# The gated stage of a fused three-layer kernel: six units of 384 tokens in place of four batches of 576 in halves of 288

## The chip, the cores and the metric

The kernel runs on one core of one Trainium2 chip. The metric is the device time of one execution in microseconds (us), the median of the runs. Engines are named as in the profile: PE is TensorE (matmuls), PEld its weight loads, DVE is VectorE, ACT is ScalarE, POOL is GpSimd, SP is the engine that issues most of the DMAs.

## The reference, cut to what matters

Three layers follow each other: an attention over 32 memory slots, a mixture of experts, and the gated layer that the change is about. There are 4 batches of 576 tokens; a token has 512 features, and the gated layer has 1024 hidden ones. `x` below is the output of the mixture of experts.

```python
h = np.maximum(x @ w_in, 0.0)                          # (4, 576, 1024)
hp = np.concatenate([zeros, h, zeros], axis=1)         # one zero row before and behind each batch
conv_out = sum(conv_w[k] * hp[:, k:k + 576, :] for k in range(3))
gate = 1.0 / (1.0 + np.exp(-conv_out))
out = h * gate @ w_out
```

The convolution runs along the tokens: a token's gate needs the hidden values of the token before it and of the token behind it in the same batch. At a batch's border the missing neighbour counts as zero.

## The kernel before

The first half (to about 205 us) computes attention and experts and leaves the experts' outputs, not yet multiplied by their gate probabilities, in DRAM (`ydram`, by batch, features on partitions, tokens along the rows; the probabilities are in `pdram`). The second half is `gated`. Nearly all products are of float32 numbers split into a high and a low part (`split`: ACT copies the high part, DVE or POOL subtracts), so each product is three matmuls (`matmul3`, L166).

`gated` walks over the 4 batches. For a batch it does the following.

- The batch's `y` (128 x 4 x 576) is loaded ahead by SP (`load_y`, L897), with the row of probabilities (`load_p`, L891). `split_y` multiplies (L905, DVE) and splits it into `yh` and `yl` (L153 ACT, L154 DVE). The pool of `y` has two buffers, `yh` and `yl` have one each, so a batch's split waits until the matmuls of the batch before have read them, and the next load but one waits for the split.
- For each of 8 groups `f` of 128 hidden features it computes `pi` = w_in x y: 4 feature blocks x 3 split terms x 2 halves of 288 tokens = 24 matmuls with 288 columns (L166). `pi` has two PSUM buffers.
- ACT takes `pi` through Relu into `ht` (L1050) and scales it into `ct` (L1052); DVE adds the two neighbours with two scalar_tensor_tensor instructions (L1053, L1055, 575 columns each); ACT takes the sigmoid (L1030); DVE multiplies (L1031, "mult" below); ACT copies the high part of `g` (L153), and DVE subtracts for the low part (L154), POOL for f = 3, 4 and 6 (`ON_POOL`). POOL also copies the last 64 tokens of the batch into `tail` (L1036), so that two batches' tails share one chunk of 128 tokens. `ht` and `ct` share 6 buffers (tag `cv`).
- The second product `po` (L1071) takes chunks of 128 tokens: 24 matmuls of 512 columns each (8 f x 3 terms). First the parts f = 0 to 5 of three chunks, then f = 6 and 7 of these, then whole chunks: 4 chunks for even batches, 5 for odd ones (the shared tail). ACT copies each chunk out (L1097), SP stores it (L1099 to L1102). The very last chunk goes into its own PSUM tile `last` and is copied out in two halves behind the branch (L1119).

The branch `tc.If(any_more > 0)` holds a second pass (`gated` with `scaled=True`) for batches in which more than one expert occurs; it isn't taken here. Instructions of one engine run in the order in which they stand in its queue. In `gated` that order is chosen at build time by a planner that simulates the engines; only the matmuls of the first batch's `pi` are kept in program order.

## Time and profile before

| | before |
|---|---|
| median of 3 runs | 411.95 us (411.86 to 412.09) |
| the profiled execution | 411.12 us |
| its span, first to last instruction | 409.4 us |
| PE busy | 401.6 us (98%) |
| DVE, ACT, POOL busy | 277.0, 221.4, 74.3 us |
| DMA | 69.04 MB, 169 GB/s in the mean |

A page of the profile has six parts; the share of busy time by engine is part 1, the span in 40 slices part 2, the costliest groups of instructions part 5. A timeline lists instructions in order of time: start, duration, engine, line, operation, output<-input, shape, and in square brackets how long the engine stood idle before it and on whom it waited. Merged rows carry a count (x12). A matmul's duration is longer than the distance to the next one, since matmuls are pipelined: for PE, the distance of starts is the cost. A table by windows lists, for each stretch, its length and each engine's busy time with the number of instructions, then the granted clock (1.00 is 2.4 GHz), the DMA share and GB/s.

### The profile page before, as it was taken

The page shows a single profiled execution, that of the slowest core. Times are in us where ns is not written, and L with a number is a line of the kernel's source. Part 1 is how long each engine was busy: PE and PEld are TensorE (multiplying, and loading weights), DVE is VectorE, ACT ScalarE, POOL GpSimd, SP SyncE. Part 2 cuts the span into 40 slices and gives each one's busy share as a digit, 9 for nine tenths or more (in the row PEclk, how much of TensorE's full clock was granted, in tenths as well). Part 3 has the DMA queues.
Part 4 walks back from the last instruction along what each step waited for, and adds up shares of the span by engine and source line. Part 5 has one row for each costly group of instructions (what it writes and reads, how often), then busy time and mean ns, then how long its engine had stood idle before and what let it go on. Part 6 is the DMA issues. An engine that isn't in the chain of part 4 may idle for free. (4 is left out here: it accounts for less than half of the span.)

```text
span 409.4 us, 8381 instructions
## 1 busy us (share of the span) xinstructions
PE 401.6 (98%) x3334; PEld 369.0 (90%) x3335; DVE 277.0 (68%) x513; ACT 221.4 (54%) x420; POOL 74.3 (18%) x123
## 2 busy tenths in 40 slices
PE   7999999999999999999999999999999999999995
PEld 6768989899998998999999988998889988999884
DVE  2679898897787986697989980688205793077600
ACT  4456567564666466465757732677215773267411
POOL 1000201402122211320102520033200232014300
PEclk9999999999999999999999999999999999999999
DMA  7999979999384949938630032000120000200022
GB/s 271 330 373 404 386 250 355 406 415 382 94 300 159 365 173 403 391 142 206 199 142 2 0 117 102 2 0 2 43 68 20 2 1 0 104 2 0 3 80 56
DMA packets 23904, 69.04 MB, mean 169 GB/s; under 512 B 3280, under 2 KB 4048, under 8 KB 23856
## 3 DMA queue, kind: packets, MB, share of 16 engines
q1 hardware_dynamic: 20272, 56.88, 38.8%
q0 software_dynamic: 3584, 11.54, 7.2%
q8 instruction: 28, 0.46, 0.4%
q14 instruction: 20, 0.16, 0.1%
HBM read 52.08 MB, written 16.33 MB: 167 GB/s over the span
## 5 line engine op out<-in xcount | busy, mean ns | idle before, releaser
L166 PE MATMUL py<-h,wb 128*128 128x288 f32 x768 | 105.3, 296 | 0.0
L166 PEld LDWEIGHTS py<-h,wb 128*128 128x128 f32 x768 | 102.4, 189 | 0.8 <-issue 0.3
L166 PE MATMUL pi<-yh,wi 128*128 128x288 f32 x512 | 90.7, 296 | 0.0
L1071 PE MATMUL po<-wo,g 128*128 128x512 f32 x360 | 84.2, 389 | 0.0
L1071 PEld LDWEIGHTS po<-wo,g 128*128 128x128 f32 x360 | 67.0, 188 | 13.1
L166 PEld LDWEIGHTS pi<-yh,wi 128*128 128x128 f32 x512 | 76.6, 189 | 0.9
L1053 DVE SCALAR_TENSOR_TENSOR ct<-ht,convw,ct 128x575 f32<-128x575 f32 x32 | 30.9, 965 | 53.0 <-ACT ct L1052 52.9
L166 PE MATMUL pi<-yl,wi 128*128 128x288 f32 x256 | 54.8, 296 | 0.0
L166 PE MATMUL ph<-att,vh 128*128 128x288 f32 x256 | 53.1, 301 | 0.2 <-DVE h L794 0.2
L1036 POOL CAST tail<-g 128x128 fp32r<-128x128 f32 x32 | 22.4, 702 | 122.7 <-DVE g L154 122.1
L878 POOL DMA_DIRECT2D ydram<-ys x32 | 17.6, 548 | 144.2 <-ACT ys L877 124.3
L166 PEld LDWEIGHTS ph<-att,vh 128*128 128x128 f32 x256 | 40.6, 188 | 3.4 <-issue 1.1
L166 PEld LDWEIGHTS pi<-yl,wi 128*128 128x128 f32 x256 | 41.2, 189 | 0.0
L1050 ACT ACTIVATE ht<-pi 128x576 f32<-128x576 f32 x32 | 20.8, 651 | 35.1 <-PE pi L166 35.1
L166 PE MATMUL ph<-att,vl 128*128 128x288 f32 x128 | 37.6, 295 | 0.0
L793 ACT ACTIVATE h<-ph 128x288 fp32r<-128x288 f32 x64 | 25.6, 408 | 17.7 <-PE ph L166 17.5
L794 DVE SCALAR_TENSOR_TENSOR h<-ph,h 128x288 fp32r<-128x288 f32 x64 | 27.9, 450 | 10.8 <-ACT h L793 10.6
L1097 ACT ACTIVATE ot<-po 128x512 f32<-128x512 f32 x17 | 9.5, 599 | 43.4 <-PE po L1071 43.4
L1031 DVE TENSOR_TENSOR ct<-ht,ct 128x576 f32<-128x576 f32 x32 | 27.2, 849 | 7.5 <-ACT ct L1030 7.5
L877 ACT ACTIVATE ys<-py 128x288 f32<-128x288 f32 x32 | 13.1, 409 | 35.4 <-PE py L166 16.4
L1055 DVE SCALAR_TENSOR_TENSOR ct<-ht,convw,ct 128x575 f32<-128x575 f32 x32 | 28.4, 887 | 0.4
L153 ACT ACTIVATE g<-ct 128x576 fp32r<-128x576 f32 x32 | 21.6, 679 | 12.6 <-DVE ct L1031 12.6
(231 smaller groups left out, 513.2 us busy)
## 6 DMA issues: line engine op xcount, KB each, us to landing
kv<-in_kv SPq DMA_DIRECT2D x16, 512.0 KB, 8.1
q<-in_q SPq DMA_DIRECT2D x8, 576.0 KB, 9.5
ydram<-ys POOLq DMA_DIRECT2D x32, 144.0 KB, 5.1
y<-ydram SPq DMA_DIRECT2D x4, 1152.0 KB, 5.8
out<-ot SPq DMA_DIRECT2D x15, 256.0 KB, 2.0
ph<-in_phi SPq DMA_DIRECT2D x8, 288.0 KB, 6.8
adram<-at POOLq DMA_DIRECT2D x8, 288.0 KB, 6.3
wa_1r<-in_w SPq DMA_DIRECT2D x4, 512.0 KB, 5.3
```

Source lines behind the costliest of these rows:

```text
L153: pin(nc.scalar.activation(hi, src, AF.Copy))
L166: pin(nc.tensor.matmul(ps, st, mv[:, cols], start=i == 0, stop=i == len(terms) - 1))
L793: nc.scalar.activation(t[:, 0, :], ps, AF.Relu)
L794: low = nc.vector.scalar_tensor_tensor(t[:, 1, :], ps, 0.0, t[:, 0, :].bitcast(F32), ALU.max, ALU.subtract)
L877: nc.scalar.activation(yt, ps, AF.Copy)
L878: stored.append(nc.gpsimd.dma_start(ydram[b, d, :, half(hf)], yt).ins)
L1031: slow(f"gm.{f}").tensor_tensor(ct, ht, ct, ALU.mult)
L1036: nc.gpsimd.tensor_copy(tail[:, f, :, to:to + 64], t[:, :, 512:576].bitcast(F32))
L1050: nc.scalar.activation(two(ht), halves(ps), AF.Relu)
L1053: nc.vector.scalar_tensor_tensor(ct[:, 1:], ht[:, :S - 1], convw[:, 0, f:f + 1], ct[:, 1:], ALU.mult, ALU.add)
L1055: nc.vector.scalar_tensor_tensor(ct[:, :S - 1], ht[:, 1:], convw[:, 2, f:f + 1], ct[:, :S - 1], ALU.mult, ALU.add)
L1071: last_product[:] = [nc.tensor.matmul(ps[:, cols], st[sp], w[:, mp, f % 2, cols], start=f == 0 and i == 0, stop=f == 7 and i == 2).ins]
```

## The change

The 4 x 576 = 2304 tokens are cut into 6 units of 384 tokens, three to every two batches. The first unit of three lies in one batch, the second crosses the border (192 tokens of each), the third lies in the second batch. A unit reads 386 columns: its 384 tokens and two neighbours (`spans`). So a unit has 8 x 12 matmuls of 386 columns in place of 8 x 24 of 288, and exactly 3 chunks of 128 tokens, with no tail. In the crossing units (1 and 4) the load is two DMAs for `y` and two for the probabilities, and each of the two DVE neighbour additions becomes two pieces of 191 or 192 columns, since tokens at the border have no neighbour across it. The last unit holds two chunks and the separate `last` tile; the hint for the branch stands behind the f = 0 to 5 parts of those two.

```diff
@@ -23,6 +23,7 @@
 B, H, S, D, M = 4, 8, 576, 64, 32
 DM, E, F = 512, 8, 1024
 HALF = S // 2
+UT, UW = 384, 386
 EPS = 1e-9
 FAR = 3e38
 
@@ -891,27 +892,36 @@
             nc.sync.dma_start(p, pdram[ds(e + 8 * b, 1), :].to_broadcast([128, S]))
             return p
 
-        def load_y(b, e):
-
-            y = state.tile([128, 4, S], F32, tag="ay", name=f"y{b}")
-            nc.sync.dma_start(y, ydram[b].rearrange("d p s -> p d s"))
-            return y, load_p(b, e, b) if e is not None else None
-
-        def split_y(b, yp, yh, yl):
+        def spans(u):
+
+            b = 2 * (u // 3)
+            return ([(b, 0, 0, UW)], [(b, 383, 0, 193), (b + 1, 0, 193, UW)], [(b + 1, 190, 0, UW)])[u % 3]
+
+        def load_y(u, scaled):
+
+            y = state.tile([128, 4, S], F32, tag="ay", name=f"y{u}")
+            p = None if scaled else late[1].tile([128, S], F32, tag="p", bufs=2, name=f"p{u}")
+            for b, at, a, z in spans(u):
+                nc.sync.dma_start(y[:, :, a:z], ydram[b].rearrange("d p s -> p d s")[:, :, at:at + z - a])
+                if not scaled:
+                    nc.sync.dma_start(p[:, a:z], pdram[ds(expert(b) + 8 * b, 1), at:at + z - a].to_broadcast([128, z - a]))
+            return y, p
+
+        def split_y(u, yp, yh, yl):
             y, p = yp
             for d in range(4):
                 if p is not None:
-                    with tc.issue_after(hidden_low[-1]) if b == 0 else contextlib.nullcontext():
-                        nc.vector.tensor_tensor(y[:, d, :], y[:, d, :], p, ALU.mult)
-                split(yh[:, d, :], yl[:, d, :], y[:, d, :])
-
-        def y_parts(b):
-            return [late[1].tile([128, 4, S], F32R, tag=t, bufs=1, name=f"{t}{b}") for t in ("yh", "yl")]
+                    with tc.issue_after(hidden_low[-1]) if u == 0 else contextlib.nullcontext():
+                        nc.vector.tensor_tensor(y[:, d, :UW], y[:, d, :UW], p[:, :UW], ALU.mult)
+                split(yh[:, d, :], yl[:, d, :], y[:, d, :UW])
+
+        def y_parts(u):
+            return [late[1].tile([128, 4, UW], F32R, tag=t, bufs=1, name=f"{t}{u}") for t in ("yh", "yl")]
 
         ys0 = []
 
         def load_first():
-            ys0.append(load_y(0, expert(0)))
+            ys0.append(load_y(0, False))
 
         def split_first():
             ys0.append(y_parts(0))
@@ -1008,99 +1018,85 @@
 
 
         def gated(gp, nm, scaled=False):
-            def first(b):
-                return None if scaled else expert(b)
 
             wo.clear()
             for j in range(4):
                 stage_out(j)
             ys = y_parts(0) if scaled else ys0[1]
             if scaled:
-                split_y(0, load_y(0, None), *ys)
-            tail = None
-            for b in range(B):
+                split_y(0, load_y(0, True), *ys)
+            for u in range(6):
                 yh, yl = ys
                 gs = []
-                if b + 1 < B:
-                    yn = load_y(b + 1, first(b + 1))
-                if b % 2 == 0:
-                    tail = gp.tile([128, 8, 2, 128], F32R, tag="tail", bufs=1, name=f"tail{b}")
-                to = 64 * (b % 2)
+                if u < 5:
+                    yn = load_y(u + 1, scaled)
+
+                o = u % 3
+                own = slice(o, o + UT)
+                lefts = ([(1, UT)], [(0, 192), (193, UT)], [(0, UT)])[o]
+                rights = ([(0, UT)], [(0, 191), (192, UT)], [(0, UT - 1)])[o]
+
                 def gate(f, ht, ct):
                     nc.scalar.activation(ct, ct, AF.Sigmoid)
-                    slow(f"gm.{f}").tensor_tensor(ct, ht, ct, ALU.mult)
-                    t = gp.tile([128, 2, S], F32R, tag="g", name=f"g{nm}{b}_{f}")
-
-                    def finish():
-                        split(t[:, 0, :], t[:, 1, :], ct, slow(f"gs.{f}"))
-                        nc.gpsimd.tensor_copy(tail[:, f, :, to:to + 64], t[:, :, 512:576].bitcast(F32))
-
+                    slow(f"gm.{f}").tensor_tensor(ct, ht[:, own], ct, ALU.mult)
+                    t = gp.tile([128, 2, UT], F32R, tag="g", name=f"g{nm}{u}_{f}")
                     gs.append(t)
-                    return finish
+                    return lambda: split(t[:, 0, :], t[:, 1, :], ct, slow(f"gs.{f}"))
 
                 before = None
                 for f in range(8):
                     fs = slice(f * 128, (f + 1) * 128)
-                    ps = banks(f"pi{b}_{f}")
-                    matmul3([(ps[:, hf, :HALF], half(hf)) for hf in range(2)],
+                    ps = banks(f"pi{u}_{f}")[:, 0, :UW]
+                    matmul3([(ps, slice(0, UW))],
                             [((wi[kc][:, 0, fs], wi[kc][:, 1, fs]), (yh[:, kc, :], yl[:, kc, :])) for kc in range(4)],
-                            tc.keep_in_program_order if b == 0 else lambda ins: ins)
+                            tc.keep_in_program_order if u == 0 else lambda ins: ins)
                     finish = gate(*before) if before else lambda: None
-                    ht = lp.tile([128, S], F32, tag="cv", name=f"ht{b}_{f}")
-                    nc.scalar.activation(two(ht), halves(ps), AF.Relu)
-                    ct = lp.tile([128, S], F32, tag="cv", name=f"ct{b}_{f}")
-                    nc.scalar.activation(ct, ht, AF.Copy, scale=convw[:, 1, f:f + 1])
-                    nc.vector.scalar_tensor_tensor(
-                        ct[:, 1:], ht[:, :S - 1], convw[:, 0, f:f + 1], ct[:, 1:], ALU.mult, ALU.add)
-                    nc.vector.scalar_tensor_tensor(
-                        ct[:, :S - 1], ht[:, 1:], convw[:, 2, f:f + 1], ct[:, :S - 1], ALU.mult, ALU.add)
+                    ht = lp.tile([128, S], F32, tag="cv", name=f"ht{u}_{f}")[:, :UW]
+                    nc.scalar.activation(ht, ps, AF.Relu)
+                    ct = lp.tile([128, S], F32, tag="cv", name=f"ct{u}_{f}")[:, :UT]
+                    nc.scalar.activation(ct, ht[:, own], AF.Copy, scale=convw[:, 1, f:f + 1])
+                    for k, by, pieces_of in ((0, -1, lefts), (2, 1, rights)):
+                        for a, z in pieces_of:
+                            nc.vector.scalar_tensor_tensor(ct[:, a:z], ht[:, o + a + by:o + z + by], convw[:, k, f:f + 1],
+                                                           ct[:, a:z], ALU.mult, ALU.add)
                     finish()
                     before = f, ht, ct
                     while len(wo) < 4 and f >= WO[len(wo)]:
                         wo.append(w2_piece(f"wo{len(wo)}", slow(f"wo.{len(wo)}")))
                 gate(*before)()
-                if b + 1 < B:
-                    ys = y_parts(b + 1)
-                    split_y(b + 1, yn, *ys)
-
-                def product(ps, c, fr, cols=slice(0, 512)):
+                if u < 5:
+                    ys = y_parts(u + 1)
+                    split_y(u + 1, yn, *ys)
+
+                def product(ps, c, fr):
                     for f in fr:
                         w = wo[f // 2].rearrange("p s (i d) -> p s i d", i=2)
-                        st = [gs[f][:, s, c * 128:(c + 1) * 128] if c < 4 else tail[:, f, s, :] for s in range(2)]
+                        st = [gs[f][:, s, c * 128:(c + 1) * 128] for s in range(2)]
                         for i, (sp, mp) in enumerate(((0, 0), (0, 1), (1, 0))):
-                            last_product[:] = [nc.tensor.matmul(ps[:, cols], st[sp], w[:, mp, f % 2, cols],
+                            last_product[:] = [nc.tensor.matmul(ps, st[sp], w[:, mp, f % 2, :],
                                                                 start=f == 0 and i == 0, stop=f == 7 and i == 2).ins]
 
-                chunks = [0, 1, 2] + [4] * (b % 2) + [3]
-                pss = {c: bank(f"po{b}_{c}") for c in chunks[:3]}
-                for c in chunks[:3]:
-                    product(pss[c], c, range(0, 6))
-                for c in chunks:
-                    if c in pss:
-                        product(pss[c], c, range(6, 8))
-                    elif b < B - 1 or c != chunks[-1]:
-                        pss[c] = bank(f"po{b}_{c}")
-                        product(pss[c], c, range(8))
-                    else:
-
-                        if not scaled:
-                            ps2_cm.__exit__(None, None, None)
-                            last_cm.append(tc.tile_pool(name="ps3", bufs=1, space=PSUM))
-                            pairs.append(last_cm[0].__enter__())
-
-                            with tc.issue_after(last_product[0]):
-                                tc.mark_branch_hint_location("more", engines=[ENG.PE])
-                            last_block.append(pairs[-1].tile([128, 512], F32, tag="last", name="last"))
-                        product(last_block[0], c, range(8))
-                        continue
-                    ot = gp.tile([128, 512], F32, tag="ot", bufs=4, name=f"ot{b}_{c}")
-                    nc.scalar.activation(ot, pss[c], AF.Copy)
-                    if c < 4:
-                        nc.sync.dma_start(out[b, c * 128:(c + 1) * 128, :], ot)
-                    else:
-                        nc.sync.dma_start(out[b - 1, 512:576, :], ot[0:64])
-                        nc.sync.dma_start(out[b, 512:576, :], ot[64:128])
-
+                pss = [bank(f"po{u}_{c}") for c in range(3 if u < 5 else 2)]
+                for c, ps in enumerate(pss):
+                    product(ps, c, range(0, 6))
+                if u == 5 and not scaled:
+
+                    with tc.issue_after(last_product[0]):
+                        tc.mark_branch_hint_location("more", engines=[ENG.PE])
+                for c, ps in enumerate(pss):
+                    product(ps, c, range(6, 8))
+                    ot = gp.tile([128, 512], F32, tag="ot", bufs=4, name=f"ot{u}_{c}")
+                    nc.scalar.activation(ot, ps, AF.Copy)
+                    at = UT * u + 128 * c
+                    nc.sync.dma_start(by_row[at:at + 128], ot)
+            if not scaled:
+                ps2_cm.__exit__(None, None, None)
+                last_cm.append(tc.tile_pool(name="ps3", bufs=1, space=PSUM))
+                pairs.append(last_cm[0].__enter__())
+                last_block.append(pairs[-1].tile([128, 512], F32, tag="last", name="last"))
+            product(last_block[0], 2, range(8))
+
+        by_row = out.rearrange("b s d -> (b s) d")
         wo, last_cm, last_product = [], [], []
         ffn_cm.__exit__(None, None, None)
         with tc.tile_pool(name="gated", bufs=8, reuse_waits="tile") as gp:
@@ -1117,7 +1113,7 @@
             cols = slice(256 * cq, 256 * cq + 256)
             ot = late[1].tile([128, 256], F32, tag="last", bufs=2, name=f"ot_{cq}")
             nc.scalar.activation(ot, last_block[0][:, cols], AF.Copy)
-            nc.sync.dma_start(out[B - 1, 384:512, cols], ot)
+            nc.sync.dma_start(by_row[B * S - 128:, cols], ot)
         last_cm[0].__exit__(None, None, None)
         late[0].__exit__(None, None, None)
 
```

## Rows read from the trace of the kernel before

**Rows 1.** The page, parts 1 and 2: busy shares, and granted clock by slice.
```profile
PE 401.6 (98%) x3334; PEld 369.0 (90%) x3335; DVE 277.0 (68%) x513; ACT 221.4 (54%) x420; POOL 74.3 (18%) x123
...
PEclk9999999999999999999999999999999999999999
```

**Rows 2.** The page, part 5: count, busy us, mean ns, idle before.
```profile
L166 PE MATMUL pi<-yh,wi 128*128 128x288 f32 x512 | 90.7, 296 | 0.0
L1071 PE MATMUL po<-wo,g 128*128 128x512 f32 x360 | 84.2, 389 | 0.0
...
L166 PE MATMUL pi<-yl,wi 128*128 128x288 f32 x256 | 54.8, 296 | 0.0
```

**Rows 3.** Timeline of PE: the start of the stage, then the last batch.
```profile
204.98 0.44 PE L166 MATMUL pi<-yh,wi 128*128 128x288 f32 x2
...
352.36 0.42 PE L166 MATMUL pi<-yh,wi 128*128 128x288 f32 x2
...
365.13 0.61 PE L1071 MATMUL po<-wo,g 128*128 128x512 f32 x2
...
378.79 15.58 PE L1071 MATMUL po<-wo,g 128*128 128x512 f32 x68
394.20 5.60 PE L1071 MATMUL po<-wo,tail 128*128 128x512 f32 x24
```

**Rows 4.** Windows, second batch, pi and product stretch: PE, PEld, DVE, ACT, POOL busy.
```profile
252.36:278.79 26.43, 26.43 (x198) 26.27 (x196) 16.79 (x21) 16.46 (x26) 5.71 (x7) 1.00 0.03 11
278.79:305.08 26.29, 26.29 (x119) 21.78 (x117) 9.40 (x13) 8.99 (x15) 4.44 (x5) 1.00 0.13 41
```

**Rows 5.** Timeline of ACT, second batch, one round: Relu, g, scaled copy, sigmoid.
```profile
268.96 0.65 ACT L1050 ACTIVATE ht<-pi 128x576 f32<-128x576 f32 x1 [1.17 <-PE pi L166]
269.51 0.67 ACT L153 ACTIVATE g<-ct 128x576 fp32r<-128x576 f32 x1
270.08 0.77 ACT L1052 ACTIVATE ct<-ht,convw 128x576 f32<-128x576 f32 x1
270.75 0.68 ACT L1030 ACTIVATE ct<-ct 128x576 f32<-128x576 f32 x1
```

**Rows 6.** Timeline of DVE, second batch: rounds, and the end of the chain.
```profile
270.22 0.76 DVE L154 TENSOR_TENSOR g<-ct,g 128x576 fp32r<-128x576 f32 x1 [0.65 <-ACT g L153]
270.89 0.81 DVE L1053 SCALAR_TENSOR_TENSOR ct<-ht,convw,ct 128x575 f32<-128x575 f32 x1
271.62 0.84 DVE L1031 TENSOR_TENSOR ct<-ht,ct 128x576 f32<-128x576 f32 x1
272.39 0.80 DVE L1055 SCALAR_TENSOR_TENSOR ct<-ht,convw,ct 128x575 f32<-128x575 f32 x1
...
277.71 1.44 DVE L1053 SCALAR_TENSOR_TENSOR ct<-ht,convw,ct 128x575 f32<-128x575 f32 x1 [0.70 <-ACT ct L1052]
...
289.00 0.76 DVE L154 TENSOR_TENSOR g<-ct,g 128x576 fp32r<-128x576 f32 x1 [0.75 <-ACT g L153]
```

**Rows 7.** Groups by shape, first half: ACT at 288 columns, DVE at 1024.
```profile
L793 ACT ACTIVATE h<-ph 128x288 fp32r<-128x288 f32 x64 | 25.6, 408 | 17.7 <-PE ph L166 17.5
...
L154 DVE TENSOR_TENSOR wi<-wi0r,wi 128x1024 fp32r<-128x1024 f32 x1 | 1.2, 1226 | 0.1
```

**Rows 8.** Timeline of POOL, second batch: a subtraction that overlaps a DVE instruction.
```profile
277.09 1.45 POOL L154 TENSOR_TENSOR g<-ct,g 128x576 fp32r<-128x576 f32 x1 [1.42 <-ACT g L153]
```

**Rows 9.** Timeline of DVE, first batch of the stage: y multiplied, first convolution.
```profile
209.74 2.77 DVE L905 TENSOR_TENSOR y<-y,p 128x576 f32<-128x576 f32 x4 [1.31 <-DMA y<-ydram]
212.43 0.81 DVE L1053 SCALAR_TENSOR_TENSOR ct<-ht,convw,ct 128x575 f32<-128x575 f32 x1
```

**Rows 10.** Timeline of SP: the load of the third y.
```profile
202.79 0.38 SPq L897 DMA_DIRECT2D y<-ydram  x1
```

**Rows 11.** Timeline of DVE, last batch: its last subtraction.
```profile
386.52 0.76 DVE L154 TENSOR_TENSOR g<-ct,g 128x576 fp32r<-128x576 f32 x1 [0.75 <-ACT g L153]
```

**Rows 12.** Timeline of ACT: copying out behind the last matmul.
```profile
405.37 0.66 ACT L1119 ACTIVATE ot<-last 128x256 f32<-128x256 f32 x2 [4.93 <-PEq L1109]
```

## The prediction

> **What bounds the kernel now.** I read the shares of busy time and the clock first [rows 1]: PE is busy 98% of the span, and the granted clock is at the upper of its two levels, 2.4 GHz, in all 40 slices. So no work on another engine, and no DMA, shortens anything unless PE waits for it; and the clock has nothing to give back. A busy PE need not be an efficient one, so next come the costliest groups [rows 2] and the timeline of PE [rows 3], read by distances of starts and not by durations. In the last batch, from 352.36 to 365.13, 96 matmuls of 288 columns start: 12.77 / 96 = 133.0 ns each. From 378.79 to 394.20, 68 matmuls of 512 columns: 15.41 / 68 = 226.6 ns each. The groups give the counts: 512 + 256 = 768 matmuls of 288 columns for `pi` (idle before them: 0.0), and 18 chunks x 24 = 432 of 512 columns for the second product (16 chunks of whole tokens and 2 shared tails). 768 x 133.0 + 432 x 226.6 = 102.1 + 97.9 = 200.0 us, against 405.37 - 204.98 = 200.4 us from the first of these matmuls to the copy behind the last one [rows 3, 12]. PE hasn't a gap of any size in this stage. The windows say the same: 26.43 of 26.43 us and 26.29 of 26.29 us [rows 4]. Only fewer columns, or less time for the same columns, can gain.
>
> **What a matmul costs beside its columns.** 288 columns at 2.4 GHz are 120.0 ns, 512 are 213.3. The rows leave 13.0 and 13.3 ns over. So, to the accuracy of the rows, a matmul costs its columns and a fixed piece of about 13 ns. The Trainium skill, "TensorE: Matmul & The Clock Gate", section "Back-to-back issue gap", gives N / 2.4 + 2.5 ns for isolated matmuls; the trace differs, with 133.0 in place of 122.5, and the measurement decides.
>
> **The matmuls of `pi`, the gain.** Removed: 768 x 133.0 = 102.1 us. Added: 6 units x 8 f x 12 = 576 matmuls of 386 columns. No row has this shape. Bounds from the two neighbours: 133.0 x 386 / 288 = 178.3 ns if all time went with columns, 226.6 x 386 / 512 = 170.8 ns if it did so from the other side; with the column rate of the granted clock, 133.0 + 98 / 2.4 = 173.8 from below and 226.6 - 126 / 2.4 = 174.1 from above. I take 173.9, since both neighbours meet there. 576 x 173.9 = 100.2 us. The columns grow by 576 x 386 - 768 x 288 = 1152 (0.5 us, the neighbours that are read twice), and 192 fixed pieces go (2.5 us): a gain of 1.9 us, between 1.8 and 2.1. What goes with the ends of the proportional bounds is 3.7 us of gain to 0.6 us of loss.
>
> **The second product.** 6 units x 3 chunks x 24 = 432 matmuls of 512 columns: the same. The copies into `tail` on POOL go; nothing but the tail's matmuls reads them, and PE had no gap there, so this is worth nothing. The stores become 18 in place of 19 issues and two half ones more; they land while PE works, except for the two last, which are as they were [rows 12].
>
> **ACT and DVE for a group f.** They gain by being off PE's path, and could lose by coming onto it: PE's time for one f falls from 24 x 133.0 = 3.19 us (for 576 tokens) to 12 x 173.9 = 2.09 us (for 384), while their instructions keep a fixed part. ACT, by distances of starts [rows 5]: 0.55 + 0.57 + 0.67, and 0.68 for the sigmoid, 2.47 us. An instruction loses 190 columns; from 576 to 288 columns the Relu goes from 0.65 to 0.41 us [rows 5, 7], so 0.16 us each: 1.83 of 2.09 us. DVE [rows 6]: 0.67 (subtraction) + 0.73 + 0.77 (mult) and 0.73 for the second neighbour addition = 2.90 of 3.19 us. A subtraction takes 1.23 us at 1024 columns and 0.76 at 576 [rows 6, 7], 1.05 ns a column, so 0.20 us less for 192 fewer. Four of these off 2.90 leave 2.10 of 2.09 us: DVE just keeps pace in the straight units. For f = 3, 4 and 6 the subtraction lies on POOL, but it stretches the DVE instruction beside it from 0.81 to 1.44 us [rows 6, 8], and comes to about the same. In the crossing units (1 and 4) two additions become four; each further one costs the fixed piece, 0.73 - 575 x 1.05 ns = 0.13 us: 2.36 us, 0.27 more than PE's step, 2.2 us late after 8 f.
>
> The Trainium skill, "VectorE: DVE Perf Modes", section "The TRN2 errata", speaks against pieces this small: a fixed cost per instruction, tiles of 512 elements or more advised. It puts VectorE's fixed part at 58 cycles; by that a round would be 1.84 us and DVE would have room. By the rows it has none.
>
> **Does PE wait for that lag?** In `pi`, PE needs for group f the PSUM buffer that the Relu of f - 2 frees. That Relu stands on ACT behind the sigmoid of f - 4, which waits for DVE. In numbers: let DVE begin the unit's first convolution t us after the unit's first matmul. Its two additions take 2 x 0.61 and two hand-overs, the sigmoid 0.42, the Relu 0.49: the Relu of f = 2 is done at t + 2.2, and PE wants its buffer at 4 x 2.09 = 8.35. So t may be 6.1 us; a microsecond more costs PE one. The lag grows little to f = 5, the last Relu that the unit's `pi` needs: about 0.2 us straight, 0.8 crossing. The unhindered t is `pi`, Relu and copy: 2.09 + 0.49 + 0.61 = 3.2 us. Before, the first batch had t = 212.43 - 204.98 = 7.45 [rows 3, 9], since DVE had stood 1.31 us for the third `y`, asked for at 202.79 [rows 10], and then multiplied it; with 4 x 3.19 us for PE and 2.9 for the longer chain, 9.9 were allowed then. Now the two products and the split ahead of that load lose 4 x 0.20 us each, and the product behind it too: t = 7.45 - 3.2 = 4.3, or 6.65 if the load lands no sooner: 0 to 0.6 us of waiting. I take 0, since the load is also a third shorter. The other first loads of a unit fall in the product stretch of the unit before, now 72 x 0.2266 = 16.3 us long.
>
> **The end of a unit.** Behind the last `pi` matmul PE has 54 matmuls (f = 0 to 5 of three chunks), of which before 4 had been pulled ahead: 50 x 0.2266 = 11.3 us. The chain of f = 7 ended 289.76 - 278.79 = 10.97 us after [rows 3, 6]. It holds 12 DVE instructions (0.20 us less each) and two ACT ones in series (0.16): 8.3 us, and 10.4 in a crossing unit. It stays hidden, by 0.9 us at the least. In the last unit only two chunks stand ahead: 32 to 36 matmuls, 7.3 to 8.2 us, where the chain took 387.28 - 378.79 = 8.49 us before [rows 3, 11] and loses 8 x 0.20 + 0.32: 6.6 us. Hidden too, by 0.7 us.
>
> **Sum.** 411.12 (the profiled execution, span 409.4 and 1.7 around it) - 1.9 = 409.2. The median of the runs is 0.83 above that execution, so 411.95 - 1.9 = 410.05, rounded to 410.1.
>
> **Rivals.** (1) PE waits once, in unit 0, with t up to the 7.45 of before: 7.45 - 6.1 = 1.35 us back, 410.1 to 411.5. For it: the third `y`'s load did end late. Against: a third less work ahead of it. (2) No gain: time goes with the columns, and the fixed piece doesn't fall with the count. The rows of `yh` now begin at multiples of 1544 bytes, and no row shows such an operand. 102.1 / 576 = 177.3 ns is the point without gain (411.95), only 3.4 ns from my price; at the proportional 178.3 ns it is 412.5. Against it: 133.0 and 226.6 lie on one line at the clock's rate. (By the rule of "TensorE: Matmul & The Clock Gate" in the Trainium skill, 768 x 122.5 and 576 x 163.3 ns are both 94.1 us, the same outcome; the trace disagrees with it already at 288 columns.) (3) Slower: DVE becomes the bound. The place is the first convolution of units 1 to 4: the multiplication of the next but one `y`, whose load can only start once the split has freed the buffer, stands ahead of it in DVE's queue. If the load lands after the product stretch, DVE starts the unit at t of 7.5 or more: 1.4 us a unit, 1.9 in crossing ones. Two such units (2.8 to 3.3) turn the gain; four give 6.5: 412.9 to 416.6. For it: DVE's 2.10 of 2.09 us leave nothing to catch up with. Against: the order on DVE is the planner's, and PE had no gap in any of the four batches.
>
> **How the numbers follow.** Forecast 0.68; (1) 0.09; (2) 0.10, half at 411.95 and half at 412.5; (3) 0.13. The range 409.5 to 412.1 holds the forecast, (1) and the half of (2). What a measurement of this kernel can tell is about 0.2%, 0.8 us. Faster by more: 0.68 + 0.06 = 0.74; within: 0.03 + 0.10 = 0.13; slower: 0.13.
>
> **What would show it.** Right: the starts of the 386-column matmuls 174 ns apart, PE without idle time from the first `pi` to the end, DVE in every unit at 2.1 to 2.4 us an f. Wrong: a distance of 177 ns or more; an idle PE at the third to sixth group of a unit, waiting for the Relu (t over 6.1); or idle PE before the f = 6 products of units 1, 4 or 5, where the cover is thinnest.

## The result: slower, 414.4 us where 410.1 was forecast

The changed kernel takes 414.36 us in the median of 22 runs (412.65 to 415.96), the kernel before 411.90 us in 22 runs beside it (410.39 to 413.09): ratio 1.0063, 95% interval 1.0049 to 1.0076. It is 2.5 us (0.6%) slower, above the range of the forecast (409.5 to 412.1). The profiled execution is 414.6 us, its span 412.8.

The page of the kernel after, parts 1 and 2 (busy time and share by engine; granted clock by slice):

```profile
PE 401.6 (97%) x3142; PEld 368.0 (89%) x3143; DVE 290.7 (70%) x619; ACT 235.2 (57%) x492; POOL 53.6 (13%) x97
...
PEclk9999999999999999999999999999999999999999
```

192 matmuls fewer, and PE is busy as long as before [rows 1]; the clock is at 2.4 GHz as before. The timeline of PE after shows the start of the stage and the first 60 matmuls with 386 columns, up to the first `po`:

```profile
206.16 0.34 PE L167 MATMUL pi<-yh,wi 128*128 128x386 f32 x1
...
216.79 2.23 PE L1076 MATMUL po<-wo,g 128*128 128x512 f32 x9
```

The distance is (216.79 - 206.16) / 60 = 177.2 ns, in later units 176.0 to 176.3, and not 173.9. That is the first loss. The stage starts 1.2 us later than in the profile of before [rows 3], but this isn't the change: a second profile of the kernel before starts at 206.85 (below).

The second loss stands at the end. The timelines of PE, ACT and SP after, from the last unit's second product on:

```profile
397.95 2.20 PE L1076 MATMUL last<-wo,g 128*128 128x512 f32 x9
399.99 1.52 PE L1076 MATMUL po<-wo,g 128*128 128x512 f32 x6
401.35 1.52 PE L1076 MATMUL last<-wo,g 128*128 128x512 f32 x6
402.71 1.52 PE L1076 MATMUL po<-wo,g 128*128 128x512 f32 x6
404.07 2.20 PE L1076 MATMUL last<-wo,g 128*128 128x512 f32 x9
```
```profile
403.82 1.09 ACT L1089 ACTIVATE ot<-po 128x512 f32<-128x512 f32 x2 [4.90 <-PE po L1076]
407.97 0.66 ACT L1115 ACTIVATE ot<-last 128x256 f32<-128x256 f32 x2 [3.06 <-ACTq L1105]
```
```profile
404.44 0.91 SPq L1091 DMA_DIRECT2D out<-ot  x2
409.22 0.81 SPq L1116 DMA_DIRECT2D out<-ot  x2
```

PE ends at 404.07 + 2.20 = 406.27, but ACT copies `last` out only at 407.97, behind a wait for its own sequencer ("ACTq") at L1105, the branch. In the kernel before, ACT stood ready, and its copy followed PE's last matmul at 405.37 [rows 12]. There the planner had put all 24 matmuls of `last` behind the other chunks, in one row:

```profile
399.64 5.60 PE L1071 MATMUL last<-wo,g 128*128 128x512 f32 x24
```

So ACT had 4.9 us between its last copy of `po` and its copy of `last`. After the change the planner wove `last` into the parts f = 6 and 7 of the two `po` chunks, and only the last 9 matmuls (2.2 us) stood behind them. What a queue needs at the branch, the instructions at L1105 after show (count; shortest, median and longest duration in ns; first and last start in us). COMPARE_BRANCH is the branch itself, EVENT_SEMAPHORE waits for a semaphore and raises it:

```profile
L1105 SPq EVENT_SEMAPHORE  x9: 17/17/17, 408.5 to 409.1; - x9
...
L1105 ACTq EVENT_SEMAPHORE  x2: 17/17/17, 407.8 to 407.9; - x2
...
L1105 ACTq COMPARE_BRANCH  x1: 50/50/50, 404.8 to 404.8; - x1
L1105 SPq COMPARE_BRANCH  x1: 53/53/53, 405.4 to 405.4; - x1
```

From the branch to the first instruction behind it are 3.0 us on ACT and 3.1 on SP, while the branch itself takes 0.05 us. Before it was 2.4 us on ACT (400.4 to 402.8) and 2.8 on SP (401.6 to 404.4), both over before PE's last matmul ended.

In these gaps the DMA part of the profile shows the queue that carries instructions at work. For the kernel after, from 404.9 to 407.7 us (packets, MB, share of 16 engines):

```profile
q14 instruction: 2, 0.02, 1.4%
```

One of the two lies before 406.5, the other behind 406.6, and the gaps of POOL (396.4 to 398.8) and DVE (399.6 to 402.4) hold one such packet each. That fits a fetch of the instructions behind the branch; that the fetch is what takes the time is not shown. Nor was a hint for ACT and SP tried: the kernel marks the branch for PE alone (`engines=[ENG.PE]`).

The account, from the profiles: first `pi` matmul to the end of the last matmul 200.26 us before and 200.11 after (forecast: 1.9 less); from there to the end of the span 4.16 before and 6.53 after (forecast: the same). -0.15 + 2.37 = +2.2, where the medians differ by 2.5. (The pages give spans to 0.1 us, so an end is good to 0.05.)

### The profile page after: what moved, and what is told of

Read it like the earlier page. It is cut to its first block, busy times and chain, and to the rows that moved or that the text cites. A ratio compares the mean times of both kernels' runs of the same rounds, so it can differ in the third digit from the quotient of the medians.

```text
span 412.8 us, 8188 instructions
## 1 busy us (share of the span) xinstructions
PE 401.6 (97%) x3142; PEld 368.0 (89%) x3143; DVE 290.7 (70%) x619; ACT 235.2 (57%) x492; POOL 53.6 (13%) x97
## 5 line engine op out<-in xcount | busy, mean ns | idle before, releaser
L167 PE MATMUL pi<-yh,wi 128*128 128x386 f32 x384 | 103.4, 338 | 0.0
L1060 DVE SCALAR_TENSOR_TENSOR ct<-ht,convw,ct 128x383 f32<-128x383 f32 (+3 forms) x128 | 67.8, 552 | 45.6 <-ACT ct L1057 44.9
L1076 PE MATMUL po<-wo,g 128*128 128x512 f32 x408 | 98.3, 390 | 0.0
L167 PE MATMUL pi<-yl,wi 128*128 128x386 f32 x192 | 64.9, 338 | 0.0
L155 POOL TENSOR_TENSOR g<-ct,g 128x384 fp32r<-128x384 f32 x18 | 19.4, 1079 | 169.7 <-ACT g L154 140.8
L1055 ACT ACTIVATE ht<-pi 128x386 f32<-128x386 f32 x48 | 23.6, 492 | 24.1 <-PE pi L167 22.9
L1041 DVE TENSOR_TENSOR ct<-ht,ct 128x384 f32<-128x384 f32 x48 | 29.4, 613 | 8.1 <-ACT ct L1040 7.5
L1040 ACT ACTIVATE ct<-ct 128x384 f32<-128x384 f32 x48 | 24.8, 516 | 14.2 <-DVE ct L1060 14.0
L154 ACT ACTIVATE g<-ct 128x384 fp32r<-128x384 f32 x48 | 24.9, 520 | 12.0 <-DVE ct L1041 12.0
L1057 ACT ACTIVATE ct<-ht,convw 128x384 f32<-128x384 f32 x48 | 29.4, 613 | 1.6
```

The costliest lines, as they stand in the source:

```text
L154: pin(nc.scalar.activation(hi, src, AF.Copy))
L155: pin((eng or nc.vector).tensor_tensor(lo, src, hi.bitcast(F32), ALU.subtract))
L167: pin(nc.tensor.matmul(ps, st, mv[:, cols], start=i == 0, stop=i == len(terms) - 1))
L1040: nc.scalar.activation(ct, ct, AF.Sigmoid)
L1041: slow(f"gm.{f}").tensor_tensor(ct, ht[:, own], ct, ALU.mult)
L1055: nc.scalar.activation(ht, ps, AF.Relu)
```

## Experiments

Two questions are asked: why a matmul costs more than forecast, and why the end is late. The recorded expectations letter their theories anew (theory B is the width in some, the late branch in others), so the text names them by what they say. "End" below is the time from PE's last matmul to the end of the span.

**A second profile of the kernel before.** 

> The kernel before, unchanged, for a second trace. The first half (to the first pi matmul) took 204.98 us in the first trace of before and 206.16 in that of after, though its instructions are the same and in the same order. If this is the spread from run to run, this trace may start pi anywhere from 204 to 207 us, with the second half still 200.3 us of PE and an end of 4.2 us. If the changed kernel slows its first half, this trace starts pi at 205.0 again.

412.98 us, span 411.2. First `pi` matmul at 206.85, end of the last at 407.11: 200.26 us again, and an end of 4.09. The start of the stage moves by 2 us from run to run, its length and its end don't. So I compare these two.

**The rows of `yh` and `yl` farther apart** (1600 bytes in place of 1544):

```diff
-[late[1].tile([128, 4, UW], F32R, ...) for t in ("yh", "yl")]
+[late[1].tile([128, 4, 400], F32R, ...)[:, :, :UW] for t in ("yh", "yl")]
```

> The changed kernel with one edit: the rows of yh and yl are 400 elements (1600 bytes) apart in place of 386 (1544 bytes); the same instructions in the same order. Theory A (where rows begin): the start-to-start time of a pi matmul falls from 177.1 to 174 ns, PE's stretch of the stage from 200.1 to 198.3 us, and the time by 1.7 us, to about 412.6. Theories B and C (width, or disturbance): 177.1 ns and the time of the changed kernel, 414.4.

414.18 us, ratio 1.0052 (1.0034 to 1.0069); the first 60 matmuls are 177.0 ns apart. So rows of 1600 bytes are no cheaper for 386 columns than rows of 1544.

**Chains of matmuls alone**, three kernels of their own. 

> A kernel of its own, which computes nothing of the reference: chains of 60 matmuls each, one bank, stationary operands that change each time in the manner of pi, nothing else running beside them. After a chain of 512 columns for warming, the chains are 512; 288 (rows 2304 bytes apart); 384 (1536 bytes); 386 (1544 bytes, as in the changed kernel); 386 (1600 bytes); 384 out of rows 1544 bytes apart; 388 (1552); 392 (1568); 400 (1600); 388 (1600); 386 (1544) again. Asked: what makes a 386-column matmul take 177.1 ns from start to start, where 386 / 2.4 + 13.3 = 174.1 was expected. Theory A, where rows begin: 386 at 1544 bytes 177, 386 at 1600 bytes 174, 384 at 1544 bytes 176, 384 at 1536 bytes 173.3. Theory B, the width (386 is no multiple of 4, 8 or 16): 386 is 177 at either distance, 384 is 173.3 at either. Theory C, other engines disturb PE in the changed kernel: all chains lie on N / 2.4 + 13.3 (386: 174.1).

> As e1_spacing, chains of 60 matmuls with nothing beside them, all out of rows 2048 bytes apart, so that only the width differs: 512, 288, 320, 352, 384, 386, 388, 400, 416, 448, 480, 512, 384, 386 (the first chain warms up, and 512, 384 and 386 stand twice). In e1_spacing 384 took 173.6 ns and 386 took 176 to 177, whatever the distance of the rows. Theory B1, a step: every width to 384 lies at N / 2.4 + 11 to 13.6 ns and every one above at 2 to 3 ns more (386: 176.5, 400: 182). Theory B2, a slope: no step, each column costs more than 1 / 2.4 ns (about 0.44 ns), so 384 is 173.6, 386 is 174.5, 512 is 230. Theory C, disturbance: all on N / 2.4 + 13.3, 512 at 226.6.

The timeline of PE in the first kernel, first matmul of its first chains behind the warming one (60 matmuls each, in the order of the expectation):

```profile
44.24 0.40 PE L49 MATMUL p<-m512h,w 128*128 128x512 f32 x1
58.24 0.29 PE L52 MATMUL p<-m288h,w 128*128 128x288 f32 x1
66.13 0.34 PE L55 MATMUL p<-m384h,w 128*128 128x384 f32 x1
76.54 0.34 PE L58 MATMUL p<-m386h,w 128*128 128x386 f32 x1
87.10 0.34 PE L61 MATMUL p386a<-m400h,w 128*128 128x386 f32 x1
97.72 0.34 PE L64 MATMUL p384o<-m386h,w 128*128 128x384 f32 x1
108.21 0.34 PE L67 MATMUL p<-m388h,w 128*128 128x388 f32 x1
```

384 columns took 173.5 ns out of rows of 1536 bytes; 386 took 176.0 out of rows of 1544 (177.0 when that chain was repeated) and 177.0 out of rows of 1600. So the row distance isn't what makes 386 columns dear. But it isn't without a price: 384 columns out of the rows of 1544 took 10.49 / 60 = 174.8, 1.3 more than out of rows of 1536. In the second kernel, all widths out of the same tiles with rows of 2048 bytes, 384 took 173.3 and 386 took 176.5. So nothing but PE is needed for the loss, and in the same tiles it depends on the width. The first matmul of its chain of 512 columns and of the chain behind it (60 matmuls apart):

```profile
25.37 0.39 PE L48 MATMUL c<-m512h,w 128*128 128x512 f32 x1
...
38.97 0.29 PE L51 MATMUL c<-m512h,w 128*128 128x288 f32 x1
```

So 512 columns took 13.60 / 60 = 226.7 ns here, where the first kernel had 14.00 / 60 = 233.3 for the same width, row distance and granted clock (1.00). There other tiles were made before this one, so its place in memory may be the reason; no run separates that. Of the widths, 352 and 400 lay on my line (13.3 and 13.5 ns over the columns), 416 and 448 above it (15.0 and 20.0), so neither a line nor one step fits. The third told rules apart:

> A kernel of its own that computes nothing of the reference: chains of 120 matmuls (three products, weights changed at each, as in the changed kernel's pi), all out of the same tiles, one width a chain. The earlier chains and the kernels gave 173.3 to 174 ns at 384 columns and 176.3 to 177.2 at 386, and 176.7 at 388. Theory S (a matmul is paid by whole steps of 8 columns, and a fixed piece of 13.3 ns on top): 378, 380, 382 and 384 all 173.3; 386, 388, 390 and 392 all 176.7; 394 and 400 both 180.0; 376 170.0; 290, 294 and 296 the same as each other. Theory L (time grows by 0.42 ns with each column, and 386 was dear by accident or by something else): 378 at 170.8, 380 at 171.7, 382 at 172.5, 386 at 174.2, 390 at 175.8. Theory P (386 is dear because it isn't a multiple of 4 or of 8, every such width pays the same extra): 380 and 388 on the line, 378, 382, 386 and 390 some 2.5 ns above it. 416, 448 and 480 are repeated: were 1.7 to 6.7 ns above the line there by accident, or again.

The timeline of PE in this third kernel, first matmul of some chains (120 matmuls each, so the distance of two successive starts / 120):

```profile
40.10 0.33 PE L48 MATMUL c<-m512h,w 128*128 128x384 f32 x1
60.92 0.33 PE L51 MATMUL c<-m512h,w 128*128 128x378 f32 x1
81.72 0.34 PE L54 MATMUL c<-m512h,w 128*128 128x392 f32 x1
103.00 0.34 PE L57 MATMUL c<-m512h,w 128*128 128x380 f32 x1
123.53 0.34 PE L60 MATMUL c<-m512h,w 128*128 128x386 f32 x1
144.73 0.34 PE L63 MATMUL c<-m512h,w 128*128 128x382 f32 x1
165.53 0.34 PE L66 MATMUL c<-m512h,w 128*128 128x390 f32 x1
```

384: 20.82 / 120 = 173.5; 378: 173.3; 386: 21.20 / 120 = 176.7; 382: 173.3. By the same reading 376 gave 173.3, 388 176.7, 390 177.8, 392 177.3, 394 180.1, 400 180.0, and 290 133.4 and 294 133.3 (288: 131.7, 296: 136.0). It is a staircase: 376, 378, 382 and 384 cost the same, 386 and 388 a step of 3.2 ns more, 394 and 400 another. That refutes the line (378 at 170.8), and the price for widths that aren't multiples of 4 or 8 (378 and 382 stand with 384). Theory S holds for the step between 384 and 386, and not for its regularity: 376 should have been 170.0, 380 is lower than its neighbours (171.1), and 416, 448 and 480 lie 15.0, 19.9 and 16.7 ns over their columns again, so that wasn't accident. What makes the stairs is open.

**384 columns in the kernel**, the neighbours left out:

```diff
-UT, UW = 384, 386
+UT, UW = 384, 384
```

> The changed kernel with pi at 384 columns in place of 386: the unit's own tokens alone, so that neighbours over a unit's border inside a batch are left out; the counts of all instructions stay. Theory B1 (a step above 384 columns): 576 x (177.0 - 173.6) = 2.0 us less for PE, of which two columns explain 0.5; the time falls from 414.4 to 412.4. Theory B2 (a slope only): 0.5 us less, 413.9. The end behind PE stays late in both.

412.36 us, ratio 1.0032 (1.001 to 1.0055). From the first `pi` matmul to the end of the last matmul 198.36 us, 1.75 less where 2.0 was expected; the end is late by as much (6.56). By distances of starts, the `pi` matmuls gave 1.5 of it (173.5 ns each in place of 176.1). The edit changes two things at once, since the rows of `yh` and `yl` are now 1536 bytes apart: by the chains, about half of the gain goes to the two columns and half to the rows (386 and 384 columns out of rows of 1544: 176.0 to 177.0 and 174.8; 384 out of 1536: 173.5).

**The last `po` chunks off ACT's queue**, three ways that failed. First copied by DVE and stored by POOL, so that ACT and SP come early to the branch:

```diff
-nc.scalar.activation(ot, ps, AF.Copy)
-nc.sync.dma_start(by_row[at:at + 128], ot)
+nc.vector.tensor_copy(ot, ps)                    # unit 5
+nc.gpsimd.dma_start(by_row[at:at + 128], ot)
```

> The changed kernel with one edit: the two chunks of the last unit that stand before the tile last are copied out by DVE in place of ACT and stored by POOL in place of SP. The order of all else on the taken path is the same. Theory of the end: ACT reads the branch only behind its copies (404.8 us) and SP behind its stores (405.4), each needs 3 us from the branch to its next instruction, so the last copy starts 1.7 us and the last store 0.9 us more late than PE allows. By it the distance from PE's last matmul to the end falls from 6.5 to about 4.2 us, as before the change, and the time by 2.3 us to about 412.0. Rival: the end is late for another reason (the stores of the last unit, or the hint for the branch on PE, which was moved): then nothing changes, 414.4, or the DVE and POOL path ends later still.

416.37 us, ratio 1.0097 (1.0068 to 1.0126). ACT's copy of `last` came right behind PE (405.91) and SP's store at 406.32, 2.9 us earlier than in the kernel after; but the program ended with POOL. Its instructions at the program's end, L1167:

```profile
L1167 POOLq DRAIN  x3: 44/107/5129, 408.7 to 414.4; - x3
```

POOL had issued two stores at 404.31, and the first drain took 5.1 us. The stores aren't the reason: that drain takes as long in the kernel after, more than 190 us behind POOL's last DMA:

```profile
L1163 POOLq DRAIN  x3: 44/107/4966, 399.0 to 412.6; - x3
```

There POOL is at the branch at 396.3, so its 2.5 us behind the branch and its 5.0 us of drain are over before PE's last matmul. Here it had waited for DVE's copies and came to the branch at 405.4. So the lateness of ACT and SP was cured, and that of POOL took its place.

Second, copied by DVE and stored by SP, the stores of `last` issued by ACT (and once more with 384 columns):

> The changed kernel with two edits at its end: the two chunks of the last unit that stand before the tile last are copied out by DVE (stored by SP, as they were), and the two stores of last are issued by ACT in place of SP. So ACT comes to the branch 6 us earlier, and what SP does behind its late branch is nothing any more. e3_branch_early showed ACT's last copy at once behind PE (405.91 us for a PE end of 405.6), but had moved the stores to POOL, whose drain then ended the kernel 5 us late. Theory of the end: last copy 0.2 us behind PE, last stores with it, the end 4.2 to 4.6 us behind PE's last matmul in place of 6.5: 412.0 to 412.4. Rival: SP's way to the kernel's end, branch and barrier, is itself the last: then the end stays at 6 us or more behind PE, and the time at 414.

> Both edits of e6_act_stores and e7_width384 in one (the neighbours over a unit's border are left out). If the step in the matmul and the late branch are all that stood between the forecast and the result, this is 414.4 - 2.0 - 2.2 = 410.2 us, what was forecast. If something else costs time in the changed kernel (DVE or ACT that can't follow), it stays at 411 or more.

413.73 us, ratio 1.005 (1.0031 to 1.007), and 412.22 with 384 columns, ratio 1.0006 (0.999 to 1.0023); ends of 6.26 and 6.18. ACT copied `last` at 406.37, but its stores went out at 409.22. SP had come to the branch at 405.5, and the last of its events behind it lies at 409.2.

Third, the stores of those two chunks moved behind the branch, copied by DVE (and with 384 columns):

```diff
+if u == 5:
+    nc.vector.tensor_copy(last_ot[c], ps)
+    continue
 ...
+for c in range(2):                               # behind the branch
+    nc.sync.dma_start(by_row[UT * 5 + 128 * c:UT * 5 + 128 * c + 128], last_ot[c])
```

> The changed kernel, but the two po chunks of the last unit are copied out of PSUM by DVE, and their stores stand behind the branch, on SP, together with those of `last`; so ACT and SP both come to the branch with nothing of the last unit's product ahead of it. Theory B2 (half of what was lost is the end: ACT and SP reach the branch so late that their first instruction behind it comes 2.4 us too late): the time from PE's last matmul to the end of the span falls from 6.5 to about 4.2 us, and the time from 414.4 to about 412.0 us, which is that of the kernel before. Rival (the end is long because of the stores' own duration, or of the branch itself, wherever the queues come to it): it stays at 6.2 to 6.5 us and 414 us.

> Both terms mended at once: 384 columns for each pi matmul (the neighbours across a unit's border are left out, so those tokens' sums lack one term) and the stores behind the branch as in the kernel with 386 columns. If the price of the matmul and the late branch are all that my sum had wrong: 198.4 us from the first pi matmul to the last matmul, 4.2 us of end, 410.1 us in all (414.4 less 2.0 less 2.3), the time I had forecast. If a third thing was missed, it stays above 411.

413.81 us, ratio 1.0052 (1.0031 to 1.0073), and 412.08, ratio 1.0003 (0.9988 to 1.0017). The ends are 6.2 and 6.6. ACT and SP now came to the branch at 398.5 and 374.1 (386 columns). The longest of SP's waits there (us in total, times, longest), and DVE's instructions at the branch, L1109:

```profile
SPq L1117 <- DVEq L1109: 29.4, 1, 29.4
```
```profile
L1109 DVEq EVENT_SEMAPHORE  x2: 21/21/21, 407.3 to 407.4; - x2
...
L1109 DVEq COMPARE_BRANCH  x1: 76/76/76, 404.4 to 404.4; - x1
```

DVE came to the branch at 404.4, behind its copy, and SP's store waited until DVE's events 2.9 us later: SP issued it at 407.37, and the stores of `last` behind it at 408.27, though ACT had copied `last` at 405.94. So my expectation failed, and not for the rival's reason, the length of the stores: it isn't enough that the queue which stores is early. In the second and the third way the last stores went out only after the events of the engine that came last to the branch, SP there and DVE here.

**The order held by hand**, which leaves the work where it is and gives it time instead: 3 matmuls of `last`, then f = 6 and 7 of the two `po` chunks, then the other 21 of `last`, all kept in program order:

```diff
+product(last_block[0], 2, range(1), tc.keep_in_program_order)
+for f in (6, 7):
+    for c, ps in enumerate(pss):
+        product(ps, c, range(f, f + 1), tc.keep_in_program_order)
 ...
-product(last_block[0], 2, range(8))
+product(last_block[0], 2, range(1, 8), tc.keep_in_program_order)
```

> The changed kernel with the order of the last unit's second product on PE written by hand: three matmuls of `last`, then the parts f = 6 and 7 of the two po chunks, then the other 21 matmuls of `last`, as the kernel before had nearly all of `last` behind the copies. Nothing is moved to another engine and no store is moved. Theory B2 (each engine that comes to the branch late loses about 3 us behind it; the planner's split of `last` made ACT and SP late): ACT copies the two chunks at about 401 us instead of 404, comes to the branch before 402 and copies `last` right behind PE's last matmul; the end falls from 6.5 to about 4.2 us and the time from 414.4 to about 412.1. Cost: if the last f's g isn't ready (DVE ended it at 399.1 in the last run), PE stalls, at most 0.5 us. Rival (the end of this kernel is longer for a reason that has nothing to do with when the queues come to the branch): 6.2 us or more, and 414 us.

> The same order of the last unit's product together with 384 columns for each pi matmul (the neighbours across a unit's border are left out, so those tokens' sums lack one term). If the price of the matmul and the late branch are all that the sum had wrong: 198.4 us from the first pi matmul to the last matmul, an end of 4.2 us, and 410.1 us in all (414.4 less 2.0 less 2.3), the time I had forecast. If a third thing was missed, it stays above 411.

411.72 us, ratio to before 0.9983 (0.9961 to 1.0004); with 384 columns 409.78, ratio 0.9934 (0.9916 to 0.9953). PE, ACT and SP at the end of the kernel with the held order and 386 columns:

```profile
398.30 2.88 PE L1076 MATMUL po<-wo,g 128*128 128x512 f32 x12
401.02 4.92 PE L1076 MATMUL last<-wo,g 128*128 128x512 f32 x21
```
```profile
400.54 1.28 ACT L1101 ACTIVATE ot<-po 128x512 f32<-128x512 f32 x2 [1.95 <-PE po L1076]
406.07 0.66 ACT L1122 ACTIVATE ot<-last 128x256 f32<-128x256 f32 x2 [4.25 <-PEq L1112]
```
```profile
401.16 1.01 SPq L1103 DMA_DIRECT2D out<-ot  x2
406.48 0.81 SPq L1123 DMA_DIRECT2D out<-ot  x2
```

ACT is at the branch at 401.8 and waits for PE again ("PEq"), not for itself; the end is 4.16 us, as in the kernel before, and PE has no idle time. That settles what made the end late: the place of the two copies in the order. With 384 columns as well, PE's first and last rows of the stage are

```profile
205.86 0.35 PE L167 MATMUL pi<-yh,wi 128*128 128x384 f32 x1
...
399.30 4.92 PE L1076 MATMUL last<-wo,g 128*128 128x512 f32 x21
```

so the stage takes 198.36 us, and the end 4.18. With both terms mended the profile is 1.9 us shorter from the first `pi` matmul on than that of before, as forecast, and the time comes out 0.3 us below the forecast. It leaves neighbours out: it is a measurement, not a kernel to use.

**The neighbours kept, two units narrower.** Units 2 and 5 take the left neighbour from a column of `ht` that POOL saved in the unit before:

```diff
+nc.gpsimd.tensor_copy(carry[:, f:f + 1], ht[:, UT:UT + 1])              # units 1, 4
+nc.vector.scalar_tensor_tensor(ct[:, 0:1], carry[:, f:f + 1], ...)      # units 2, 5
```

> The kernel with the held order, and the left neighbour of units 2 and 5 isn't read and multiplied a second time: POOL keeps the last column of each ht of units 1 and 4, and DVE adds it with one further instruction of one column; so these two units have 384 columns and the other four keep 386. By the step measured between 384 and 386 columns (3.2 ns) it saves 2 x 96 x 3.2 = 0.6 us of PE: 411.1 us where the held order gave 411.7. Rival: the 16 further instructions on POOL and the 16 on DVE (some 0.2 us each) cost PE a wait, since DVE had 2.10 us of work for PE's 2.09 in a straight unit: 411.7 or above.

411.47 us, ratio to before 0.9988 (0.997 to 1.0007). The stage took 200.12 us in its profile, against 200.11 with the held order alone: the 0.6 us aren't there, and PE has no idle time that would have taken them. The unbroken run of 57 matmuls in unit 5:

```profile
372.20 0.34 PE L167 MATMUL pi<-yh,wi 128*128 128x384 f32 x1
...
382.15 1.53 PE L1085 MATMUL po<-wo,g 128*128 128x512 f32 x6
```

9.95 / 57 = 174.6 ns, where the held order had 176.3; in unit 2 it is 175.3 for 176.0. The expectation priced these matmuls at the step measured elsewhere, but they read 384 columns out of rows that stay 1544 bytes apart, and for that the first chains had 174.8 and not 173.5. So the two units gave some 0.2 us in place of 0.6. The second product took 0.2 more (98.86 us for 98.66 by distances of starts); why is open. This kernel and the one with the held order are the best that keep the whole computation: both under the changed kernel, and neither to be told from the kernel before.

## Why the prediction was wrong, point by point

**What bounds the kernel: right for the stage.** PE has no gap in it after the change either, and the clock stayed at its upper level. It isn't right for the 4.2 us behind PE's last matmul: there the time hangs on when ACT and SP are past the branch, though PE waits for neither.

**What a matmul costs beside its columns, and the matmuls of `pi`: the term that was mis-sized.** The two rows, 133.0 ns at 288 columns and 226.6 at 512, lay on a line, and I read 173.9 off it for 386. It is 176.0 to 177.2: between the two widths PE pays in uneven steps, and 386 lies two columns behind one. By distances of starts summed over the stage, the 576 matmuls of `pi` took 101.4 us and the 768 of before 102.1: a gain of 0.7, where 1.9 was forecast. The lesson is in my own bounds: I had 170.8 to 178.3 from the proportional ends, then took a line through two points for knowledge, though rival 2 said that no row shows the shape and that 3.4 ns more would eat it all. It got one chance in ten. What I had named for it, the row distance, wasn't what made 386 columns dear; it costs 1.3 ns at 384.

A smaller piece: the second product, forecast as the same, took 98.7 us after and 98.1 before by the same sums. 0.5 us; no run shows why. In the chains 512 columns took 226.7 or 233.3 ns from one kernel to the other, so the price of this form isn't fixed either.

The Trainium skill, "TensorE: Matmul & The Clock Gate", section "Back-to-back issue gap", writes the distance of isolated warm matmuls as N / 2.4 + 2.5 ns, a line too. The chains here show 10.8 to 20.0 ns over the columns, in steps; the measurement decides.

**The second product, "the two last are as they were": the step that failed.** I counted the issues of the stores and took over their place. The place depends on an order that the planner chooses anew. Before, the whole of `last` stood behind the copies and ACT waited 4.93 us for PE there [rows 12]; after, 9 of its 24 matmuls stood there. That wait was the slack that hid the way past the branch, and the prediction, which cites the row for "as they were", put it at nothing. What the runs showed: from the branch 3.0 us on ACT and 3.1 on SP to the next instruction, and an end of 6.53 us in place of 4.16; the order held by hand brings 4.16 back. Price: 2.4 us.

**ACT and DVE, the lag, the end of a unit: right.** DVE's first convolution began 3.8 us behind the first matmul of unit 0 (209.91 - 206.16), and 5.6 to 5.7 in the other five, where 6.1 were allowed. (There the planner had put 3 to 7 of the unit's matmuls ahead, between those of the product before; behind the start of the unbroken run it is 2.4 to 3.0.) Rivals 1 and 3 (a wait in unit 0, DVE as the bound) are refuted by that and by PE without idle time. The chain of the last f ended at about 399.5 (ACT's copy of g at 398.39, DVE's subtraction behind it), and PE took up those parts at 402.71.

**The sum.** 410.05 forecast, 414.36 measured: 4.3 missed, of which 1.75 on PE (200.11 against 198.36 with 384 columns, the price I had assumed) and 2.4 at the end. The kernel with both mended gives 409.8. None of my rivals held the end; the half of rival 2 that I priced at 411.95 would have been right without it.

## What to carry to other kernels

A line through two widths is no price for a third: time a chain of the very shape before the width is fixed, and where there is a choice, stay at the low side of a step (384, not 386), with the rows at the distance that you timed. And when a change lets a planner order the last stretch anew, read who waits for whom at the end before and after: an idle wait ahead of a branch or of the last store may be what hides a fixed delay, and holding the order by hand there gave back the 2.4 us of the end (medians 414.36 and 411.72).

## What the runs showed of the hardware that I had not expected

- The distance of matmuls of float32 pairs at the upper clock goes in uneven steps with the width. Out of rows of 2048 bytes 376, 378, 382 and 384 columns took 173.3 to 173.5 ns, 386 and 388 176.7, 394 and 400 180.0 to 180.1; 448 columns are dear (206.6 ns, 19.9 over the columns).
- The same width isn't always the same price: 384 columns took 173.5 ns out of rows of 1536 bytes and 174.8 out of rows of 1544, and 512 columns took 226.7 and 233.3 in two kernels with the same row distance.
- A branch that takes 0.05 to 0.08 us is followed by 2.4 to 3.7 us without an instruction on ACT, SP, DVE and POOL. The Trainium skill, "Runtime: NRT & Kernel Launch", section "Instruction fetch mechanics", says that a branch to a far target makes the engine wait for its instructions to be fetched; the trace agrees in that there is a gap, and that the instruction queue moves a packet in it; that the packet is the cause isn't shown.
- POOL's first drain at the end of the program takes 5.0 us in the kernels before and after, more than 180 us behind POOL's last DMA, and 5.1 us where POOL had issued two stores 4.4 us before. It costs time only where POOL comes late to it.
